# Replanning ScalarE and VectorE in a statically scheduled kernel: room kept for copies, held sums, earlier sines

## The chip, the cores and the metric

The kernel runs on one core of one Trainium2 chip. The metric is device time in microseconds (us) of one execution; lower is better. Executions are with the TensorE clock granted in full (0.999 to 1.0).

## The reference, cut to what matters

Two branches act on the same normalised input and are added to it: a state space layer (S5) with a linear recurrence over 2048 steps, and a gated MLP with a spatial product `w_sp @ z2`.

```python
xn = layernorm(x)                                    # x: 1 x 2048 x 640
# branch A: h[t] = Lam_bar * h[t-1] + B_bar @ xn[t]  (complex, 640 states)
#           y = 2 Re(C h) + xn * Dskip
# branch B: z = gelu(xn @ w_in); z1, z2 = halves of z (864 columns each)
#           z2 = layernorm(z2);  g = w_sp @ z2 + b_sp   (w_sp: 2048 x 2048)
#           out = (z1 * g) @ w_out
return x + y + branchB
```

## The kernel before

The kernel does not write its instructions in order. It records operations with what they read and write and with an expected duration. A list scheduler then fixes, before the program exists, each engine's order. That order stays as planned. In these traces an engine whose next instruction must wait does not take a later one first: below, VectorE stands idle for 3.22 us before one instruction. TensorE's order is given; that of ScalarE, VectorE and the load queue is planned.

```python
# the scheduler's choice (cut): of what can start soonest, the one with the longest tail
s0 = min(max(f, o.rdy) for o in lst)
cand = max((o for o in lst if max(f, o.rdy) <= s0 + (self.EPS0 if s0 < self.TEPS else eps)),
           key=lambda o: o.tail)
...
if op.nbytes:
    if op.lat > 2.2:                      # a transposing load
        dma_free = max(st + 1.25, dma_free) + op.nbytes / 270e3
        free[eng] = st + 0.65 + op.nbytes / 300e3
```

The products use Strassen's scheme: sums of blocks on VectorE, seven products on TensorE, and PSUM results handed on through copies on ScalarE. In the spatial stage (`W @ z2`, eight steps j) TensorE accumulates several products into one bank and needs a copy of the bank in between (shortened; each `prod` is eight matmuls, each copy an operation on ScalarE):

```python
prod(X, "A11", "B11", True, "P1")
act(copy bank X -> bank Z)                       # p1_j: P6 may not enter X before it has run
prod(Y, "S1", "T1", True, "P5")
ev(f(p5), Y, ...)                                # p5_j: P3 needs Y free
prod(X, "S2", "T2", False, "P6")
ev(f(u2), X, b0, ...)                            # u2_j: P7 may not enter X before it has run
prod(Z, "A12", "B21", False, "P2")
prod(X, "S3", "T3", False, "P7")
ev(f(u3), X, b1, ...)                            # u3_j
...
```

In the same stretch ScalarE also has to scale C (`cy`), for VectorE's products (`cp`), and the states (`P`, `Q`, `h7`), for VectorE's fixes of the recurrence (shortened):

```python
def c_scale(held):                               # at j = 3; q = 0..4
    ta, tb = cy_m[q % 2 * 2], cy_m[q % 2 * 2 + 1]     # cy of q+2 needs the buffer that cp of q reads
    act(ta = k2 * im)    # cy{q}0
    act(tb = k2 * re)    # cy{q}1
    dve(re = re * k1 + ta)   # cp{q}0
    dve(im = im * k1 - tb)   # cp{q}1
...
act(pv = sc * hv)        # P{q}{j}, Q{q}{j}: need the scan of q and its negated copy (shn{q}) from VectorE
```

The sums of blocks of W for the first step, and the sines that the recurrence needs:

```python
def s_comb(j):                                   # on VectorE
    tt(S3, a11, a21, ALU.subtract, "S3")
    tt(S1, a21, a22, ALU.add, "S1")
    tt(S2, S1, a11, ALU.subtract, "S2")
    tt(S4, a12, S2, ALU.subtract, "S4")
...
act(sins, [Civ("an"), u_m.iv()], [Civ("rn"), sin_m.iv(), cos_m.iv()], ..., "sins")
```

## Time and profile before

| | before |
|---|---|
| time, median of 3 runs | 262.41 us (262.28 to 262.89) |
| profiled execution | 262.98 us, span 260.7 us |
| TensorE busy | 256.1 us (98%) |
| first and last matmul start | 1.19 and 258.15 us |
| TensorE stalls before 30 us / after 100 us | 3.73 / 1.27 us |

"Stall" here and below means: the distance between two successive matmul starts in the trace, less N/2.4 + 2.5 ns for N columns. That is the rate which the Trainium skill gives for a warm array ("TensorE: Matmul & The Clock Gate", section "Wait — 56ns, not 53.3ns?"), and this trace agrees: 432-column matmuls follow each other every 182.5 ns and 512-column ones every 216 ns. The exception is the start: the first seven matmuls (512 columns, on zeros) follow each other every 0.40 to 0.43 us, though the granted clock reads 1.00 there. So about 1.2 us of each figure "before 30 us" is their slower pace and no wait that the change could remove. "After 100 us" sums the gaps of 0.1 us and more; "before 30 us" is all the rest. Without stalls the matmuls of this kernel take 251.97 us from the first start to the last. So the span is 1.19 us, plus 251.97 us, plus the stalls, plus a tail of about 2.56 us.

These are the busy times and the chain of work that ended last, from the page of the kernel before:

```profile
PE 256.1 (98%) x1500; PEld 151.5 (58%) x1500; DVE 243.9 (94%) x567; ACT 179.6 (69%) x323; POOL 26.0 (10%) x50
...
DVE 49%; PE 36%; POOL 4%; issue 4%; DMA 3%; ACT 1%; SPq 1%; DVEq 0%
```

TensorE is busy nearly always, but half of the chain runs through VectorE: TensorE is waiting for something that hangs on VectorE. The list "who waited for whom" of the kernel before, from 100 to 258 us, weight loads (PEld) only; columns are total us, times, longest us:

```profile
PEld ps L1079 <- ACT arena L1092: 1.6, 3, 0.7
PEld ps L1079 <- ACT ps L1101: 0.7, 1, 0.7
PEld ps L1234 <- ACT ps L1256: 0.3, 1, 0.3
PEld ps L1227 <- ACT ps L1256: 0.2, 1, 0.2
```

L1079 is the spatial product. L1101 is the copy p1 and L1092 the copies u2, c11, u3 and c21. The timeline of ScalarE at the first of these stalls (columns: start us, duration us, engine, line, operation, out<-in, count, and in brackets the idle time before and its releaser):

```profile
152.68 0.83 ACT L992 ACTIVATE arena<-arena 128x640 bf16<-128x640 bf16 x1 [0.47 <-DVE arena L997]
153.42 0.51 ACT L1101 COPY ps<-ps 128x432 f32<-128x432 f32 x1
```

ScalarE waited 0.47 us for VectorE's C product (L997), then scaled C (L992, cy20), and only then made the copy p1_4 that TensorE needed. And why VectorE was late (timeline of VectorE):

```profile
49.11 1.33 DVE L731 TENSOR_SCALAR arena<-arena 128x864 bf16<-128x864 bf16 x3
53.66 1.29 DVE L1034 TENSOR_TENSOR arena<-arena 128x1024 bf16<-128x1024 bf16 x2 [3.22 <-DMA arena<-in_B_w_sp_dram]
...
56.46 0.75 DVE L788 SCALAR_TENSOR_TENSOR arena<-arena 128x512 f32<-128x512 bf16 x1
```

It stood 3.22 us before the first sum of W (L1034), for the load of W. The recurrence (L788) began only behind that sum.

### The profile page before, as it was taken

To read this page: it belongs to the slowest core of one execution; us is meant where nothing else is said; L and a number is where in the kernel's file an instruction comes from. 1 tells how busy PE (TensorE), PEld (TensorE's weight loads), DVE (VectorE), ACT (ScalarE), POOL (GpSimd) and SP (SyncE) were. 2 spreads that over 40 slices of the span, in tenths; PEclk is the share of its full clock that TensorE was granted. 3 is DMA by queue.
4 is the path that set the end of the run, shared out by engine and by line. 5 is a ranking of instruction groups with operands and counts; after the bars stand their busy time and mean duration, and the time that the engine had idled before them with its cause. 6 is when DMAs were issued, how large, how long until landed. Compare 5 with 4: busy or idle time off the path is not lost.

```text
span 260.7 us, 4329 instructions
## 1 busy us (share of the span) xinstructions
PE 256.1 (98%) x1500; PEld 151.5 (58%) x1500; DVE 243.9 (94%) x567; ACT 179.6 (69%) x323; POOL 26.0 (10%) x50
## 2 busy tenths in 40 slices
PE   7999999999999999999999999999999999999996
PEld 3455554444446777755555544455557677777774
DVE  5899999679999999999999999999999999999953
ACT  6899999989986544533242595873979897884110
POOL 3467065400000000000000000000000000000000
PEclk9999999999999999999999999999999999999999
DMA  7946699999706962399989867893133555545641
GB/s 195 317 117 119 138 148 208 225 303 237 116 10 119 163 234 102 134 323 176 247 197 198 227 150 186 195 197 99 43 113 97 148 134 131 142 128 151 154 141 54
DMA packets 90324, 42.49 MB, mean 163 GB/s; under 512 B 73054, under 2 KB 90302, under 8 KB 90302
## 3 DMA queue, kind: packets, MB, share of 16 engines
q1 hardware_dynamic: 89982, 42.09, 67.5%
q8 instruction: 12, 0.20, 0.3%
q10 hardware_dynamic: 320, 0.12, 0.2%
q14 instruction: 10, 0.08, 0.1%
HBM read 12.28 MB, written 12.45 MB: 95 GB/s over the span
## 4 chain that ended last, share of the span: by engine, by line
DVE 49%; PE 36%; POOL 4%; issue 4%; DMA 3%; ACT 1%; SPq 1%; DVEq 0%
PE ps L1227 23%; PE ps L1079 10%; DVE arena L788 9%; DVE arena L793 5%; DVE arena L1034 5%; DVE arena L810 5%; DVE arena L790 5%; DVE arena L1013 3%; DVE arena L645 2%; DVE arena L647 2%; DVE arena L1120 2%; POOL arena L602 2%; DMA arena<-in_A_x_dram 2%; PE ps L1234 2%; DVE arena L1099 2%
## 5 line engine op out<-in xcount | busy, mean ns | idle before, releaser
L1079 PE MATMUL ps<-arena 128*128 128x432 bf16 x448 | 82.6, 346 | 0.5 <-ACT arena L1092 0.2
L1079 PEld LDWEIGHTS ps<-arena 128*128 128x128 bf16 x448 | 43.5, 98 | 39.4 <-ACT arena L1092 1.6
L1227 PE MATMUL ps<-arena 128*128 128x320 bf16 (+2 forms) x456 | 64.6, 296 | 0.0
L865 ACT ACTIVATE arena<-arena 128x512 bf16<-128x512 bf16 x70 | 46.3, 712 | 11.2 <-DVE arena L869 9.2
L1227 PEld LDWEIGHTS ps<-arena 128*128 128x128 bf16 x456 | 44.1, 98 | 17.1 <-ACT ps L1256 0.2
L665 PE MATMUL ps<-arena 128*128 128x432 bf16 x280 | 51.9, 346 | 0.1
L665 PEld LDWEIGHTS ps<-arena 128*128 128x128 bf16 x280 | 34.6, 124 | 16.4 <-DMA arena<-arena 0.5
L759 PE MATMUL ps<-arena 128*128 128x512 bf16 x200 | 43.3, 379 | 0.0
L759 PEld LDWEIGHTS ps<-arena 128*128 128x128 bf16 x200 | 19.6, 98 | 23.5 <-DMA arena<-arena 0.2
L1092 ACT ACTIVATE arena<-ps,arena 128x432 f32<-128x432 f32 (+1 forms) x32 | 19.6, 616 | 19.7 <-PE ps L1079 18.7
L788 DVE SCALAR_TENSOR_TENSOR arena<-arena 128x512 f32<-128x512 bf16 x35 | 25.7, 750 | 0.0
L764 ACT CAST arena<-ps 128x512 bf16<-128x512 f32 x40 | 22.3, 600 | 3.6 <-PE ps L759 3.5
L1034 DVE TENSOR_TENSOR arena<-arena 128x1024 bf16<-128x1024 bf16 x32 | 21.2, 691 | 3.2 <-DMA arena<-in_B_w_sp_dram 3.2
L869 DVE TENSOR_TENSOR arena<-arena 128x1024 bf16<-128x1024 bf16 (+1 forms) x42 | 24.2, 597 | 0.0
L743 ACT ACTIVATE arena<-ps 128x864 bf16<-128x864 f32 x16 | 14.2, 891 | 14.0 <-PE ps L665 11.1
L1248 DVE TENSOR_TENSOR arena<-ps,arena 128x320 bf16<-128x320 f32 (+1 forms) x40 | 18.6, 483 | 4.3 <-PE ps L1234 3.2
L810 DVE TENSOR_TENSOR arena<-arena 128x512 f32<-128x512 f32 (+2 forms) x40 | 21.6, 559 | 0.0
L1256 ACT COPY ps<-ps 128x320 f32<-128x320 f32 x24 | 9.9, 413 | 16.1 <-PE ps L1227 16.1
L793 DVE SCALAR_TENSOR_TENSOR arena<-arena 128x256 bf16<-128x256 bf16 (+1 forms) x35 | 16.8, 484 | 0.0
L790 DVE SCALAR_TENSOR_TENSOR arena<-arena 128x256 bf16<-128x256 bf16 (+1 forms) x35 | 16.8, 481 | 0.0
L1194 DVE TENSOR_TENSOR arena<-arena 128x640 bf16<-128x640 bf16 x32 | 15.3, 484 | 0.0
L1175 DVE TENSOR_TENSOR arena<-arena 128x384 bf16<-128x384 bf16 x32 | 11.1, 352 | 0.5 <-DMA arena<-g_scratch 0.5
(118 smaller groups left out, 255.4 us busy)
## 6 DMA issues: line engine op xcount, KB each, us to landing
g_scratch<-arena SPq DMA_DIRECT2D x16, 224.0 KB, 2.6
z_scratch<-arena SPq DMA_DIRECT2D x16, 216.0 KB, 1.9
arena<-z_scratch SPq DMA_DIRECT2D x8, 432.0 KB, 4.0
arena<-in_A_x_dram SPq DMA_DIRECT2D x16, 160.0 KB, 3.6
base_scratch<-arena SPq DMA_DIRECT2D x16, 160.0 KB, 2.3
arena<-base_scratch SPq DMA_DIRECT2D x16, 160.0 KB, 2.7
out_dram<-arena SPq DMA_DIRECT2D x15, 160.0 KB, 2.4
arena<-in_B_w_in_dram SPq DMA_DIRECT2D x8, 216.0 KB, 3.9
```

The costliest lines, as they stand in the source:

```text
L665: r = e.matmul(ps[:, b + h, 0:FG], lhs(k), winv[:, k, hcol * FH + h * FG:hcol * FH + (h + 1) * FG], start=(k == 0), stop=(k == ND - 1))
L759: r = e.matmul(ps[:, b, :], btv[:, ri, k, q * 128:(q + 1) * 128], xnTv[:, k, tq * 512:(tq + 1) * 512], start=(k == 0), stop=(k == ND - 1))
L764: act(lambda e: e.copy(o[:, ri, tq], ps[:, b, :].rearrange("p (m j) -> p j m", j=8)), [bank(b)], [l_m.iv((q * 8 + j) * 1024 + ri * 512 + t ...
L788: dve(lambda e: e.scalar_tensor_tensor(tv, prev, lr, cur, op0=ALU.mult, op1=ALU.add), pr + [l_iv(q, j)] + cr, [t.iv()], cd(512) + PTR, nm ...
L790: dve(lambda e: e.scalar_tensor_tensor(dst[:, 0:256], prev[:, 256:512], nli, tv[:, 0:256], op0=ALU.mult, op1=ALU.add), pr[1:2] + cr + [t.i ...
L793: dve(lambda e: e.scalar_tensor_tensor(dst[:, 256:512], prev[:, 0:256], li, tv[:, 256:512], op0=ALU.mult, op1=ALU.add), pr[0:1] + cr + [t. ...
L810: tt = lambda o, a, b, op: (lambda e: e.tensor_tensor(o, a, b, op))
L865: act(lambda e, pv=pv, hv=hv, lo=lo, sc=sc: e.activation(pv, hv[:, lo:lo + 2, 1:257], ACT.Identity, scale=sc), [h.iv(), Civ(cn)], [m.iv((q ...
L869: dve(lambda e, mv=mv, lq=lq: e.tensor_tensor(lq, lq, mv, ALU.add), li + [m.iv(0, 1024 * n)], li, cd(512 * n, 2), "fix%s%d%d" % (nm, q0, j))
L1034: dve(lambda e: e.tensor_tensor(o.ap(1024), x.ap(1024), y.ap(1024), op), [x.iv(), y.iv()], [o.iv()], cd(1024, 2), "%s_%d" % (name, j))
L1079: r = e.matmul(ps[:, bk, 0:FG], lv_[:, k, :], rv[k], start=(first and k == 0), stop=(k == 7), skip_group_check=True)
L1227: r = e.matmul(ps[:, bk, c0:c1], lf(q), rf(q)[:, c0:c1], start=(first and q == 0), stop=(q == 7), skip_group_check=True)
```

## The change

It changes no arithmetic and no instruction count; it changes orders. A second planning pass knows when each ScalarE copy for TensorE will be ready, and refuses to start another ScalarE operation that would run over it (`keep`). Operations of VectorE and ScalarE that wait for another engine are taken as ready 0.8 us later than computed (`LOOSE`). The queue time of transposing loads is set to measured values. The first sums of W may not run before the third product of the recurrence (`S_HELD`). The sines get a bias that puts them ahead of the squares, and B u takes its first token blocks later.

```diff
--- before.py
+++ after.py
@@ -31,6 +31,7 @@
 
 
     EPS0 = 0.12
+    LOOSE, LOOSE_BY = ("cy", "P", "Q", "h7", "fix"), 0.8
     TEPS = 12.0
     DMA_LAT = 2.0
     DMA_BW = 280e3
@@ -85,14 +86,29 @@
         out.sort(key=lambda s: s[0])
         self.mem[space] = out
 
+    KEEP_T0, KEEP_BY, KEEP_SLACK = 100.0, 0.25, 1.2
+
     def schedule(self):
-        ops = self.ops
-        last_pe = None
-        for op in ops:
+
+        for op in self.ops:
             for p in op.preds:
                 p.succs.append(op)
+        self.keep = []
+        self.plan()
+        for op in self.ops:
+            if op.eng == "act" and op.start > self.KEEP_T0:
+                sl = [s.start - op.done for s in op.succs if s.eng == "pe"]
+                if sl and min(sl) < self.KEEP_SLACK:
+                    self.keep.append((op.rdy, op))
+        return self.plan()
+
+    def plan(self):
+        ops = self.ops
+        keep = dict((o, r) for r, o in self.keep)
         pe = [o for o in ops if o.eng == "pe"]
         nxt = {a: b for a, b in zip(pe, pe[1:])}
+        for op in ops:
+            op.start = -1.0
         for op in reversed(ops):
             t = 0.0
             for s in op.succs:
@@ -130,6 +146,23 @@
                     cand = pe[pei]
                     st = max(f, cand.rdy)
                 else:
+                    if eng == "act" and keep:
+                        held = {}
+                        for o in lst:
+                            t = max(f, o.rdy)
+                            if o not in keep:
+                                for k, r in keep.items():
+                                    if k.start < 0 and t < r + 0.05 and t + o.occ > r + self.KEEP_BY:
+                                        t = r + k.occ
+                                        break
+                            held[o] = t
+                        s0 = min(held.values())
+                        lst2 = [o for o in lst if held[o] <= s0 + eps]
+                        cand = max(lst2, key=lambda o: o.tail)
+                        st = max(f, cand.rdy, s0 if cand not in keep else 0.0)
+                        if best is None or st < best[0]:
+                            best = (st, cand)
+                        continue
                     s0 = min(max(f, o.rdy) for o in lst)
                     cand = max((o for o in lst if max(f, o.rdy) <= s0 + (self.EPS0 if s0 < self.TEPS else eps)), key=lambda o: o.tail)
                     st = max(f, cand.rdy)
@@ -145,7 +178,7 @@
             if op.nbytes:
                 if op.lat > 2.2:
                     dma_free = max(st + 1.25, dma_free) + op.nbytes / 270e3
-                    free[eng] = st + 0.65 + op.nbytes / 300e3
+                    free[eng] = st + {163840: 1.28, 819200: 3.6}.get(op.nbytes, 1.45)
                     op.done = dma_free + 2.2
                 else:
                     at = max(st + op.occ + 0.9, dma_free)
@@ -158,6 +191,8 @@
             for s in op.succs:
                 s.npred -= 1
                 at = op.start + op.occ if eng == "pe" == s.eng else op.done
+                if eng != s.eng and s.eng in ("act", "dve") and s.name.startswith(self.LOOSE):
+                    at += self.LOOSE_BY
                 if at > s.rdy:
                     s.rdy = at
                 if s.npred == 0:
@@ -515,10 +550,11 @@
         ACTM = (0, 1, 3)
         LNE_DVE = (5, 6, 7)
         HELD = ()
-        XNB = 0.0
+        XNB = 5.0
         XN_AFTER = (6, 7, 8, 9)
         ACT_Z2 = (8, 12)
         NHALF = 4
+        SINS = 20
         XT_ACT = (6,)
         BT_AT, BT_DEP = 10, 11
         LASTN = 480
@@ -935,7 +971,7 @@
                 e.activation(C("rn"), C("an"), ACT.Sin, scale=6.2831845)
                 e.activation(s_, u, ACT.Sin, scale=-6.2831845)
                 return e.activation(c, u, ACT.Sin, scale=3.1415925)
-            act(sins, [Civ("an"), u_m.iv()], [Civ("rn"), sin_m.iv(), cos_m.iv()], 1.3 + 0.2 + 2 * 1.34 + 1.3, "sins")
+            act(sins, [Civ("an"), u_m.iv()], [Civ("rn"), sin_m.iv(), cos_m.iv()], 1.3 + 0.2 + 2 * 1.34 + 1.3, "sins", bias=SINS)
             act(lambda e: e.activation(c, c, ACT.Square, scale=math.sqrt(2.0)), [cos_m.iv()], [cos_m.iv()], ca(1280) + 0.15,
                 "tsq")
             act(lambda e: e.activation(c, c, ACT.Copy, scale=-1.0, bias=1.0), [cos_m.iv()], [cos_m.iv()], ca(1280) + 0.1,
@@ -1017,6 +1053,7 @@
             dve(tt(tv[2], b21, tv[0]), i21 + ti[0], ti[2], cd(FH, 2), "T4_%d" % n)
 
         scnt = [0]
+        S_HELD = {0: [l_iv(0, 3)]}
         s_of = {}
 
         def s_comb(j):
@@ -1031,7 +1068,7 @@
             a11, a12, a21, a22 = [w_of[(j, n)] for n in ("A11", "A12", "A21", "A22")]
 
             def tt(o, x, y, op, name):
-                dve(lambda e: e.tensor_tensor(o.ap(1024), x.ap(1024), y.ap(1024), op), [x.iv(), y.iv()], [o.iv()],
+                dve(lambda e: e.tensor_tensor(o.ap(1024), x.ap(1024), y.ap(1024), op), [x.iv(), y.iv()] + S_HELD.get(j, []), [o.iv()],
                     cd(1024, 2), "%s_%d" % (name, j))
             tt(S3, a11, a21, ALU.subtract, "S3")
             tt(S1, a21, a22, ALU.add, "S1")
@@ -1361,9 +1398,10 @@
         dve(lambda e: e.tensor_copy(bsp_m.ap(16, FP32), bsb_m.ap(16)), [bsb_m.iv()], [bsp_m.iv()], 0.08, "bsp")
         for q in range(5):
             for ri in range(2):
-                for qq in ((0, 1) if q == 0 else (q,) if q > 1 else ()):
-                    for tq in (1, 2, 3, 0):
-                        bu(qq, tq, ri)
+                for tqs in (((1, 2, 3), (0,)) if q == 0 and ri == 0 else ((1, 2, 3, 0),)):
+                    for qq in ((0, 1) if q == 0 else (q,) if q > 1 else ()):
+                        for tq in tqs:
+                            bu(qq, tq, ri)
             if q < 4:
                 t_comb(2 * q)
             for j in range(1, 8):
```

## The prediction

> **What bounds the kernel.** TensorE. It is busy 256.1 of 260.7 us, but busy time of pipelined matmuls overstates, so I read start-to-start times. Those of 432 columns follow each other every 182.5 ns, of 512 every 216 ns, of 320 every 136 ns: the N/2.4 + 2.5 ns that the Trainium skill gives for a warm array ("TensorE: Matmul & The Clock Gate", section "Wait — 56ns, not 53.3ns?"), which this trace shows. What exceeds that rate sums to only 5.0 us. Of it 3.4 us lie before 17 us, 0.2 us at 21.0 us, about 1.3 us in the second half. A tail of about 2.5 us follows the last matmul. The clock is granted in full. So the change can only win part of the 1.3 us; the start it hardly touches.
>
> **The five stalls in the second half** (the timeline): +0.39 us at 153.98, +0.19 at 157.10, +0.18 at 160.21, +0.40 at 167.92, +0.11 at 207.84; together 1.27 us. In "who waited for whom" they are weight loads of the W z2 products waiting for ScalarE's copies out of PSUM (1.6 us over 3 waits, and 0.7 us once). The cause: ScalarE did a C-scaling activation (0.82 us) first. At 152.68 it starts one, 0.47 us late for want of VectorE's C product; TensorE's copy starts only at 153.42. VectorE is late because the first sum of W waited 3.2 us for the load of W around 50 to 54 us, and is never idle from 60 to 240 us to make it good.
>
> **What the change does** (instruction order per engine; none added or removed).
> - ScalarE: three C-scalings and many state scalings P, Q and h7 move behind the copies TensorE waits for. This should remove most of the four W z2 stalls (1.16 us) and the last (0.11 us).
> - VectorE: the first sums of W now stand more than 8 us later, among the recurrence. The 3.2 us wait should vanish, and VectorE runs about 3 us earlier. That only restores the slack of the C products.
> - ScalarE: the sines (2.59 us, with a table load of 1.28 us, which agrees with "ScalarE: Activation LUTs", section "What ACT_TABLE_LOAD costs") move from 47 to about 42 us. They block PSUM copies about 3.9 us; eight banks at 1.08 us each absorb that. No TensorE time.
> - B u reorder: the first tokens' tiles are needed about 3 us later. No stall stands there, so no time.
>
> **Sum:** about −1.1 us of 1.27 us. 262.4 − 1.1 = **261.3 us**, range **260.7 to 262.3**. Faster by over 2%: 1%; within 2%: 98%; slower by over 2%: 1%.
>
> **What shows it right or wrong.** TensorE's matmul starts: the gaps near 154, 157, 160 and 168 us gone, the start of the output stage about 1.2 us earlier, the last matmul near 257 us. VectorE's wait for the load of W at 50 to 54 us gone. TensorE's waits for ScalarE's copies down from about 2.6 us to under 0.6 us. Busy times unchanged; TensorE between 40 and 110 us unchanged.
>
> **What would make it wrong.** The held copies leave ScalarE idle and push P and Q so late that VectorE's fixes miss the output products: then new stalls from 188 us on. Or the W sums, held too long, make the first spatial products late at about 110 us. Or the earlier sines starve B u of banks near 42 to 46 us. Or the start varies by more between executions than the gain (before varies by 0.6 us).

## The result, and the profile after

| | before | after |
|---|---|---|
| median of 6 runs, same rounds | 262.74 us (262.28 to 263.15) | 261.31 us (261.25 to 261.60) |
| ratio | | 0.995 (95%: 0.9937 to 0.9963) |
| profiled execution, span | 260.7 us | 259.4 us |
| TensorE stalls before 30 us | 3.73 us | 3.70 us |
| TensorE stalls after 100 us | 1.27 us | 0.00 us |
| first 320-column matmul (output stage) | 192.75 us | 191.59 us |
| last matmul start | 258.15 us | 256.85 us |

A ratio is the mean time of one kernel's runs over that of the other's of the same rounds, so it is not quite the ratio of the medians. The two profiled spans differ by 1.30 us, and the stalls by 1.27 + 0.03 us: the whole difference between these two executions is stall time of TensorE, nearly all of it after 100 us. (Four of the 200 matmuls of B u are missing from the trace of after; the four gaps of exactly one matmul that this leaves are not counted.)

The same two lines of the page of after:

```profile
PE 255.2 (98%) x1496; PEld 152.4 (59%) x1500; DVE 244.3 (94%) x567; ACT 179.8 (69%) x323; POOL 26.3 (10%) x50
...
PE 95%; DMA 3%; SPq 0%; DVE 0%; issue 0%
```

The busy share of TensorE is the same 98% as before; the chain tells the difference, because it now runs through TensorE alone. The list of waits of after has no wait of TensorE or its weight loads from 100 to 258 us, so there is nothing to show. ScalarE near 152 us in after: the copy (L1138) is ahead of the C scaling (L1028).

```profile
152.37 0.50 ACT L1138 COPY ps<-ps 128x432 f32<-128x432 f32 x1
152.78 0.83 ACT L1028 ACTIVATE arena<-arena 128x640 bf16<-128x640 bf16 x1
```

VectorE near 50 us in after: the wait for W is gone, and the recurrence (L824) starts at 51.44 us, 5.0 us earlier than before.

```profile
49.10 1.32 DVE L767 TENSOR_SCALAR arena<-arena 128x864 bf16<-128x864 bf16 x3
50.35 0.16 DVE L997 TENSOR_SCALAR arena<-arena 128x5 f32<-128x5 f32 x1
...
51.44 0.75 DVE L824 SCALAR_TENSOR_TENSOR arena<-arena 128x512 f32<-128x512 bf16 x1
```

### The profile page after: what moved, and what is told of

It is laid out like the page before. It is cut to its first block, busy times and chain, and to the rows that moved or that the text cites. A ratio compares the mean times of both kernels' runs of the same rounds, so it can differ in the third digit from the quotient of the medians.

```text
span 259.4 us, 4334 instructions
## 1 busy us (share of the span) xinstructions
PE 255.2 (98%) x1496; PEld 152.4 (59%) x1500; DVE 244.3 (94%) x567; ACT 179.8 (69%) x323; POOL 26.3 (10%) x50
## 4 chain that ended last, share of the span: by engine, by line
PE 95%; DMA 3%; SPq 0%; DVE 0%; issue 0%
PE ps L1116 32%; PE ps L1264 23%; PE ps L701 18%; PE ps L795 17%; PE ps L722 3%; DMA arena<-arena 2%; PE ps L1271 2%; DMA arena<-in_B_w_in_dram 2%; SPq L409 0%; PE ps L659 0%; DVE arena L675 0%; DVE arena L643 0%; DVE arena L1329 0%; DVE arena L633 0%
## 5 line engine op out<-in xcount | busy, mean ns | idle before, releaser
L824 DVE SCALAR_TENSOR_TENSOR arena<-arena 128x512 f32<-128x512 bf16 x35 | 25.7, 743 | 0.0
L1285 DVE TENSOR_TENSOR arena<-ps,arena 128x320 bf16<-128x320 f32 (+1 forms) x40 | 18.0, 482 | 5.3 <-PE ps L1271 3.6
L1231 DVE TENSOR_TENSOR arena<-arena 128x640 bf16<-128x640 bf16 x32 | 14.6, 482 | 0.0
L715 ACT ACTIVATE arena<-arena 128x864 bf16<-128x864 bf16 x12 | 11.1, 922 | 0.0
```

The lines of the kernel that those rows point to most:

```text
L824: dve(lambda e: e.scalar_tensor_tensor(tv, prev, lr, cur, op0=ALU.mult, op1=ALU.add), pr + [l_iv(q, j)] + cr, [t.iv()], cd(512) + PTR, nm ...
L1285: dve(lambda e: e.tensor_tensor(o[0][:, c0:c1], ps[:, bk, c0:c1], y[0][:, c0:c1], ALU.add), [bank(bk), y[1]], [o[1]], cd(c1 - c0), "%s_%d" ...
```

## The experiments

The prediction blamed ScalarE's order for the stalls, with VectorE's lateness as what had upset it. Three theories can be told apart. A: ScalarE's order alone makes the stalls. B: VectorE's lateness alone makes them. C: a stall needs both, an instruction ahead of the copy, and a VectorE late enough to hold that instruction up. Twelve kernels were run, all correct, on three chips. Each has its own runs of the kernel before (11 each), because chips may differ.

The orders were edited after planning. The helper below moves named operations in one engine's list, and then recomputes the start times, from which the waits are made:

```python
def swap(self, e, moves):
    l = self.order[e]
    for what, after in moves:
        a = next(o for o in l if o.name == what)
        l.remove(a)
        l.insert(1 + next(i for i, o in enumerate(l) if o.name == after), a)
    self.refit()
```

### Summary

The last column is the ratio to before, with its 95% interval. "Start" and "late" are TensorE's stalls before 30 us and after 100 us in the one profiled execution. "C product" is the start of VectorE's first C product, a measure of VectorE's lateness.

| kernel | chip | start | late | C product | median us | ratio to before |
|---|---|---|---|---|---|---|
| before, first profile | | 3.73 | 1.27 | 151.77 | 262.74 | |
| before again | 2 | 3.81 | 0.37 | 150.96 | 262.25 | 0.9986 (0.9959 to 1.0012) |
| before, four ScalarE moves | 1 | 3.82 | 1.49 | 152.04 | 262.29 | 1.0008 (0.9982 to 1.0033) |
| before, three VectorE moves | 1 | 3.72 | 0.33 | 150.78 | 262.27 | 1.0003 (0.9976 to 1.0030) |
| before, hold alone | 1 | 3.39 | 0.74 | 149.96 | 261.94 | 1.0001 (0.9972 to 1.0029) |
| before, sines and B u alone | 3 | 3.46 | 1.39 | 151.79 | 263.36 | 1.0033 (1.0002 to 1.0063) |
| after, first profile | | 3.70 | 0.00 | 150.28 | 261.31 | 0.995 (0.9937 to 0.9963) |
| after again | 2 | 3.92 | 0.00 | 150.51 | 261.70 | 0.9982 (0.9943 to 1.0021) |
| after a third time | 3 | 3.84 | 0.00 | 150.43 | 261.32 | 0.9951 (0.9924 to 0.9977) |
| after, one sum of W early | 1 | 3.31 | 0.85 | 151.83 | 262.58 | 1.0016 (0.9990 to 1.0041) |
| after, no room kept | 2 | 3.36 | 0.26 | 150.71 | 262.10 | 0.9988 (0.9961 to 1.0016) |
| after, no hold | 2 | 3.83 | 0.00 | 150.36 | 262.32 | 0.9986 (0.9960 to 1.0012) |
| after, sines late | 3 | 3.63 | 0.00 | 150.30 | 261.79 | 0.9982 (0.9948 to 1.0016) |
| after, tile 7 first | 3 | 3.19 | 0.00 | 149.77 | 261.12 | 0.9944 (0.9918 to 0.9969) |

The medians of before were 261.86, 262.57 and 262.39 us, with ranges of 2.1 to 2.4 us. The intervals reach about 0.26% or more to each side, so differences of under about 0.7 us between timed kernels are not established by the times; the stalls are one execution each.

The time of the C product still contains TensorE's own progress, which differs at the start. A cleaner measure of VectorE's lateness is how long after the end of ScalarE's first two C scalings VectorE begins the C product. It is 0.04 to 0.18 us in seven kernels: hold alone, the three profiles of after, no hold, sines late, tile 7 first. It is 0.62 to 0.89 us in three (three VectorE moves, before again, no room kept) and 1.61 to 2.05 us in four (before, four ScalarE moves, sines and B u alone, one sum early). The late stalls are none in the first group (0.74 us in hold alone, for a reason of its own, given in its section), 0.26 to 0.37 us in the second and 0.85 to 1.49 us in the third.

### Four ScalarE moves in the kernel before

```diff
         g.schedule()
+        g.swap("act", (("cy20", "p1_4"), ("cy31", "u2_4"), ("cy41", "u3_4"), ("Q10", "u2_5")))
```

> The kernel before with four ScalarE instructions moved one place (cy20 behind p1_4, cy31 behind u2_4, cy41 behind u3_4, Q10 behind u2_5) and nothing else. Theory A (ScalarE's order makes the four stalls): the TensorE stalls at 154, 157, 160 and 168 us go, 1.16 us in sum, and the time is 1.0 to 1.2 us under before, although VectorE's first sum of W still waits about 3.2 us for the load of W. Rival B (VectorE's lateness makes them): the stalls stay within 0.3 us of their 1.16 us, because nothing of VectorE has changed.

Measured: the copy p1_4 is now ahead (L1126 ahead of the C scaling L1017), and the three stalls at 154 to 160 us are gone although VectorE still waited 3.25 us for W. ScalarE in this kernel:

```profile
152.43 0.50 ACT L1126 COPY ps<-ps 128x432 f32<-128x432 f32 x1
152.97 0.83 ACT L1017 ACTIVATE arena<-arena 128x640 bf16<-128x640 bf16 x1
```

But the late stalls are 1.49 us, not 0.1, and the time is that of before. The lost time moved on. Here is the next meeting point at 164 to 168 us, first in the kernel before, then in this one. L830 and L855 are VectorE's negated state (shn0), L865 and L890 ScalarE's state scalings that need it, L1090 and L1115 the copy p5_5, L1092 and L1117 the copy u2_5.

```profile
164.12 0.23 DVE L830 TENSOR_SCALAR arena<-arena 128x256 bf16<-128x256 bf16 x1
...
164.38 1.33 ACT L865 ACTIVATE arena<-arena 128x512 bf16<-128x512 bf16 x2 [0.54 <-DVE arena L830]
...
165.63 0.50 ACT L1090 COPY arena<-ps 128x432 f32<-128x432 f32 x1
...
167.26 0.60 ACT L1092 ACTIVATE arena<-ps,arena 128x432 f32<-128x432 f32 x1
...
167.92 0.90 PE L1079 MATMUL ps<-arena 128*128 128x432 bf16 x4 [0.24 <-ACT arena L1092]
```

```profile
164.39 0.24 DVE L855 TENSOR_SCALAR arena<-arena 128x256 bf16<-128x256 bf16 x1
...
164.67 1.34 ACT L890 ACTIVATE arena<-arena 128x512 bf16<-128x512 bf16 x2 [1.51 <-DVE arena L855]
...
165.91 0.50 ACT L1115 COPY arena<-ps 128x432 f32<-128x432 f32 x1
...
166.93 0.61 ACT L1117 ACTIVATE arena<-ps,arena 128x432 f32<-128x432 f32 x1
...
167.60 1.09 PE L1104 MATMUL ps<-arena 128*128 128x432 bf16 x5 [0.60 <-ACT arena L1117]
```

VectorE delivers its state at about the same time in both. TensorE and ScalarE arrive 0.7 us earlier in this kernel, because they lost nothing at 154 to 160 us, and so they wait longer: ScalarE's idle time before the state scaling grows from 0.54 to 1.51 us, and the stall near 168 us from 0.40 to 0.76 us (the brackets of the PE lines give 0.24 and 0.60 us, because the ends of matmuls are modelled; the stalls are read from the starts). Two later stalls (0.26 and 0.18 us) follow in the same stage. Theory A falls as an account of the sum, while it is right about the first three stalls. Theory B's wording falls too, since those three went without any change to VectorE; but the sum stayed, as B expected.

### Three VectorE moves in the kernel before

```diff
         g.schedule()
+        g.swap("dve", (("S1_0", "h06a"), ("S2_0", "h07c"), ("S3_0", "S2_0")))
```

> The kernel before with three VectorE instructions moved (the first three sums of W for j=0, into the recurrence) and nothing else; ScalarE's order is that of before. Theory A (order alone): the 3.2 us wait for W goes, VectorE is about 2.7 us earlier, and the four stalls stay at about 1.16 us. Rival B (lateness alone) and theory C (both are needed: the old order fits a VectorE that is on time): the stalls fall under 0.3 us and the time is 1.0 to 1.2 us under before.

Measured: no wait for W; the late stalls are 0.33 us (0.20 at 166.95 and 0.13 at 206.89 us) with ScalarE's old order untouched. VectorE is earlier by 1.0 us at the C product, not by the 2.7 us expected, because it now idles for ScalarE's sines and copies at 51 to 53 us. That was enough. The time did not fall in the runs (ratio 1.0003), so the mechanism is seen here in the trace and not in the timed runs. This contradicts theory A and agrees with B and C alike; what speaks against B alone is the kernel with the four ScalarE moves. ScalarE in this kernel, with the C scaling (L1017) still ahead of the copy p1_4 (L1126):

```profile
152.11 0.82 ACT L1017 ACTIVATE arena<-arena 128x640 bf16<-128x640 bf16 x1
152.83 0.52 ACT L1126 COPY ps<-ps 128x432 f32<-128x432 f32 x1
```

### One sum of W early in the kernel after

The reads that hold the four sums back are dropped after planning, and the first sum is moved. Nothing else of any order differs from after.

```diff
         g.schedule()
+        for op in g.ops:
+            if op.name in ("S1_0", "S2_0", "S3_0", "S4_0"):
+                op.preds = {p: True for p in op.preds if p.name[:2] not in ("h0", "u0")}
+        g.swap("dve", (("S1_0", "z2n7"),))
```

> The kernel after with one VectorE instruction (the first sum of W) moved back before the recurrence, so that VectorE again waits about 3 us for the load of W; ScalarE's order stays that of after. Theory A and C: ScalarE's new order bears the late VectorE, the stalls near 154 to 168 us stay under 0.3 us in sum, and the time is within 0.4 us of after. Rival B (lateness alone): the stalls come back, about 1.2 us, and the time is that of before.

Measured: VectorE stands idle before that sum again; the profile names no DMA as releaser here ("issue"), but the trace has the third load of W landing at 52.31 us, 0.08 us before the sum starts.

```profile
52.39 0.69 DVE L1096 TENSOR_TENSOR arena<-arena 128x1024 bf16<-128x1024 bf16 x1 [2.18 <-issue]
```

The C product is at 151.83 us, as late as in before. Around 154 to 168 us only 0.15 us is lost, so there the new ScalarE order does bear the late VectorE, as A and C expected. But 0.70 us is lost after 187 us, at the output products waiting for ScalarE's copies, which no theory had expected, and the median is 0.7 us over before's of that call. Keeping room helps where the planner saw the risk; it does not make the plan proof against a late VectorE.

### The hold alone, in the kernel before

```diff
+        S_HELD = {0: [l_iv(0, 3)]}
...
-[x.iv(), y.iv()], [o.iv()],
+[x.iv(), y.iv()] + S_HELD.get(j, []), [o.iv()],
```

> The kernel before with only the hold on the first sums of W, through the scheduler (which replans ScalarE and VectorE around it). Theory B and C: stalls of the second half under 0.4 us, time 0.9 to 1.3 us under before. Theory A: stalls stay about 1.2 us unless the new plan happens to move the same copies.

Measured: no wait for W, and the earliest C product of all kernels of this call (149.96 us). Still 0.74 us of late stalls, 0.60 of it at 166.98 us. The scheduler had replanned everything around the hold: in the new order VectorE's negated state is ready at 165.04 us, later than in before (164.35 us). VectorE was on time at the C product. But shortly ahead of the negated state stands a product with z1, and it waited 1.04 us for a store to g_scratch:

```profile
163.62 0.61 DVE L1121 TENSOR_TENSOR arena<-arena 128x864 bf16<-128x864 bf16 x1 [1.04 <-DMA g_scratch<-arena]
```

In before the product at this place (L1120, at 163.27 us) did not wait. So VectorE can become late by another transfer than the load of W. One part of a plan cannot be judged by itself when the planner reacts to it. This run fits none of the expectations cleanly; it agrees with the finding that the late stalls follow the moment at which VectorE delivers what ScalarE has queued ahead of a copy.

### After, before, and two parts left out, on the second chip

After and before were run again unchanged.

> The kernel after once more, unchanged, beside the kernel before. If the gain of 1.3 to 1.4 us is the change's own: ratio 0.993 to 0.997, spread of its runs under 0.6 us, no TensorE stall after 100 us in its profile. If it was the luck of one chip or of the runs of before: ratio 0.998 to 1.002 and a spread of 1 us or more, as the kernels of the first call showed (before alone ranged from 261.14 to 263.40 us there).

> The kernel before once more, as a kernel of its own: a second profile and more runs. Ratio 0.999 to 1.001. If the stalls of the second half belong to the plan: about 1.3 us of them again near 154 to 168 us. If they depend on how late the load of W lands in an execution: another sum, larger where the first sum of W starts later than 53.7 us and smaller where it starts earlier.

Measured: after again has no late stall. Its median is 0.87 us under that of before, but one of its six runs took 264.08 us, so the interval reaches 1.0021, and the expected ratio and spread were missed; the other five lie between 261.36 and 262.14 us. Nothing shows what happened in that one run. Before again is the more instructive one. It has only 0.37 us of late stalls, and its wait for W is 2.25 us:

```profile
52.86 1.29 DVE L1034 TENSOR_TENSOR arena<-arena 128x1024 bf16<-128x1024 bf16 x2 [2.25 <-DMA arena<-in_B_w_sp_dram]
```

The program is identical to the one that lost 1.27 us. VectorE came 0.8 us earlier to its C product (150.96 against 151.77 us), and the three stalls at 154 to 160 us did not occur; the one at 167 us was 0.26 in place of 0.40 us. The load that ended the wait is the third transposing load of W, here first in before and then in before again:

```profile
50.09 1.31 SPq L372 DMA_TRANSPOSE arena<-in_B_w_sp_dram  x1
```

```profile
49.39 1.31 SPq L372 DMA_TRANSPOSE arena<-in_B_w_sp_dram  x1
```

From issue to landing it took 3.55 and 3.45 us. So 0.70 of the 0.80 us were lost before its issue: earlier transposing loads had held the queue longer (one near 37 us for 2.27 us against 1.70 us).

So the 1.27 us on which the prediction rested belonged to one execution in which W came late, not to the kernel as such. Three executions with before's ScalarE order now line up: C product at 150.78, 150.96 and 151.77 us, late stalls of 0.33, 0.37 and 1.27 us.

The kernel after without the hold, and the kernel after with one planning pass:

```diff
-        S_HELD = {0: [l_iv(0, 3)]}
+        S_HELD = {}
```

> The kernel after without the hold on the first sums of W; ScalarE still plans in two passes and keeps room. If the hold matters: VectorE waits 2 to 3.5 us for the load of W again, stalls after 100 us of 0.5 to 1.3 us, time 0.5 to 1.3 us over after. If keeping room is enough: stalls under 0.3 us and the time of after.

Measured: no late stall, and no wait for W either. The planner, which starts the sines early and knows the load times, has put the first recurrence product (51.36 us) ahead of the first sum of W (53.00 us) by itself. The hold is not needed to remove the wait. The timed runs were no better than before's (262.32 us), which the profile does not explain: its tail is 2.88 us against 2.56 us in after again, and its start is within 0.1 us. The next kernel's tail is 3.11 us; in all three VectorE's last instruction ends 0.55 us after the last matmul start, so the longer tails come after the arithmetic.

```diff
-        return self.plan()       # second pass, with room kept
+        return self.order
```

> The kernel after with a single planning pass, so that ScalarE again puts p1_4, u2_4, u3_4 behind the C-scalings; the sums of W are still held, so VectorE is on time. If VectorE's lateness was the cause: stalls after 100 us under 0.4 us, time within 0.4 us of after. If ScalarE's order was: about 1 us of stalls and the time of before.

Measured: 0.26 us of late stalls, at 195.98 us. ScalarE's three C scalings stand ahead of the copies again, as in before, and yet no stall occurs at 154 to 168 us, because VectorE is nearly on time (C product at 150.71 us, 0.89 us after the scalings):

```profile
151.78 0.82 ACT L1028 ACTIVATE arena<-arena 128x640 bf16<-128x640 bf16 x1
152.50 0.52 ACT L1138 COPY ps<-ps 128x432 f32<-128x432 f32 x1
```

This is the plainest answer to the question of cause: the old order of p1_4, u2_4 and u3_4, with a VectorE that is not far behind, costs nothing there. The 0.26 us is all that the second pass can have been worth between these two executions.

### The sines

Sines, B u order and the small bias alone, on the kernel before; and the kernel after with the sines where they were:

```diff
# sines and B u alone (on before)
-        XNB = 0.0
+        XNB = 5.0
...
-..., "sins")
+..., "sins", bias=20)
# and the B u loop of the change
# sines late (on after)
-        SINS = 20
+        SINS = 0
```

> The kernel before with only the earlier sines, the B u order and the small bias on the early transposes. What has been seen so far: the stalls after 100 us follow VectorE's lateness (before: wait for W 3.22 us, stalls 1.27 us; before again: 2.25 us, 0.37 us). If the sines are what starts VectorE's recurrence early: its first product starts near 52 to 54 us in place of 55.6 to 56.5, the first sum of W still stands before it and still waits 1 to 3 us, stalls after 100 us 0.2 to 0.8 us. If they do nothing: the stalls of before.

> The kernel after without the bias that puts the sines ahead of the squares; hold, room for copies and the new load times stay. The recurrence cannot start before the sines have ended (about 51 us), so its first product starts near 54 us, 2.5 us later than in after (51.4 to 52.1), with VectorE idle some 2 us before it. If VectorE's lateness decides: stalls after 100 us of 0.3 to 1.2 us, the time 0.3 to 1.2 us over after. If ScalarE's kept room decides: none, the time of after.

Measured, alone: the recurrence starts earlier (53.65 us), but the first sum of W still stands ahead of it and waits 1.62 us, and VectorE reaches the C product at 151.79 us, as late as before. With TensorE 0.3 us further along than in before, because it lost less at the start, the stall at 154 us is 0.74 us and the late stalls 1.39 us, above the 0.2 to 0.8 us expected. The times are 0.3% longer than before. Measured, in after with the sines late: no late stall, the C product at 150.30 us. VectorE idled only 0.8 us for the sines, and the planner had reordered the rest. So the early sines are neither enough nor needed. The sines themselves cost TensorE nothing: no kernel has a stall between 30 and 100 us. Here is ScalarE's table load for them, in before and then in after:

```profile
47.03 1.28 ACT L935 ACT_TABLE_LOAD   x1
48.32 0.27 ACT L935 ACTIVATE arena<-arena 128x80 f32<-128x80 f32 x1
```

```profile
41.92 1.28 ACT L971 ACT_TABLE_LOAD   x1
43.21 0.27 ACT L971 ACTIVATE arena<-arena 128x80 f32<-128x80 f32 x1
```

### A third time after, and an attempt to beat both

With no late stall left, what remains is the start. In every profile so far TensorE waited near 21 us for the transposing load of tile 7, by 0.07 to 0.73 us (the expectation quoted below overstates the least of them). Two neighbouring VectorE instructions are swapped in after, so that tile 7 is normalised before tile 5 is copied:

```diff
         g.schedule()
+        g.swap("dve", (("xnT5", "xn7"),))
```

> The kernel after a third time, as the measure for the other three of this call: no stall after 100 us in its profile, ratio to before 0.994 to 0.999, median 0.3 to 1.5 us under before.

> An attempt to beat both: the kernel after with two neighbouring VectorE instructions swapped near 16 us, so that the normalised tile 7 is ready about 0.4 us earlier and its transposing load is issued about 0.4 us earlier. TensorE waits 0.32 to 0.73 us at 21.0 us for that load in every run so far. Expected: that stall falls by 0.3 to 0.4 us, none appears at 17 us, the time is 0.2 to 0.4 us under after. If the load's landing is set by other traffic and not by its issue: no change.

TensorE around 21 us in after, third profile; the load (SPq) is the transpose of tiles 7 to 9, and the matmuls that wait are those of tile 7:

```profile
16.23 5.47 SPq L407 DMA_TRANSPOSE arena<-arena  x3
...
16.74 3.82 PE L701 MATMUL ps<-arena 128*128 128x432 bf16 x20
...
21.17 0.72 PE L701 MATMUL ps<-arena 128*128 128x432 bf16 x3 [0.60 <-DMA arena<-arena]
```

And with tile 7 first:

```profile
15.94 6.48 SPq L432 DMA_TRANSPOSE arena<-arena  x4
...
16.86 4.92 PE L726 MATMUL ps<-arena 128*128 128x432 bf16 x26
```

The matmuls run through without a gap. The stall of 0.77 us at 21.2 us (0.32 us in the first profile of after) is gone, none appeared at 17 us, and the start stalls are 3.19 us, the smallest of all kernels. The six runs have a median of 261.12 us against 261.32 us of after on the same chip, with overlapping ranges (260.86 to 261.35, and 260.76 to 261.72). The trace agrees with the gain, and so do the times, but neither proves it: in the thirteen other profiles, without the swap, this stall already ranged from 0.07 to 0.77 us. Of all kernels run this one has the lowest median.

## Why the prediction was right

**The bound and the size.** The forecast was 261.3 us; measured was 261.31 us. TensorE was the limit, 1.27 us of its stalls were all that the second half could give, the change removed all of them, and the start changed by 0.03 us. In the repeats the medians differed by 0.87 and 1.07 us. The exact hit has luck in it: the forecast started from 262.41 us, and before's median in the rounds of the result was 262.74 us.

**The signs.** The last matmul moved from 258.15 to 256.85 us, the output stage began 1.17 us earlier, the wait for W vanished, and TensorE's waits for ScalarE's copies after 100 us went to none. The first two were foretold within 0.2 us, and the last was under the forecast's 0.6 us. TensorE was unchanged between 40 and 110 us.

**Where the reasoning was off: the step "three C-scalings and many state scalings P, Q and h7 move behind the copies TensorE waits for. This should remove most of the four W z2 stalls".** By itself it does not. Four such moves in the kernel before took away three stalls and paid for them at the next place where ScalarE has VectorE's work queued ahead of a copy (0.76 us in place of 0.40 us at 167.6 us; 1.49 us in all). With VectorE nearly punctual, such an order cost 0.33 us in one kernel and 0.26 us in another. VectorE's lateness is what is lost; ScalarE's order decides where TensorE feels it. The prediction named the lateness as the cause behind, but gave it no worth of its own ("That only restores the slack").

**"VectorE runs about 3 us earlier".** It was 1.5 us at the C product and 2.6 us at the negated state (164.12 to 161.52 us), because VectorE also has idle time early on (1.45 us near 46 us in after, where before had 1.08 us) and its order is another. What the C product could gain was bounded as well: in after it starts 0.09 us after ScalarE's scalings, so VectorE had no more than this to win there.

**The hold.** The wait for W vanished as foretold, but the hold is not its only remedy: without it, the new plan has no wait either. With several remedies that replace each other, leaving one out shows little. The kernel after without the hold and that with the sines late both kept every late stall away.

**Variation.** The prediction took the stalls of one profile for those of the kernel. They vary: 1.27 and 0.37 us in two executions of the same program, with waits for W of 3.22 and 2.25 us. How much of the 0.87 to 1.43 us between the medians was late stalls in the runs without a profile is therefore not shown. The profiled execution of before was 262.98 us, near the slow end of its runs, so the stalls were at the high end too. After has shown none in three profiles. What part of the remaining spread of run times comes from the start (stalls of 3.2 to 3.9 us there in the profiles) is not settled, nor are the single runs of about 264 us.

## What to carry to other kernels

In a fixed order of instructions, removing one stall behind a late engine may only move the loss to the next place where its work is queued ahead of what the bottleneck needs (here 1.27 us of stalls became 1.49 us). Find the earliest idle time of the engine that is late, and give it other work there. And before you take a sum of small stalls from one profile, take a second profile of the same kernel: when the sum hangs on when the queue reaches a load, it belongs to the execution.

## What the Trainium skill lacked or had wrong

- "TensorE: Matmul & The Clock Gate", section "Wait — 56ns, not 53.3ns?", agrees with every run here after the first 6 us, for 320, 432 and 512 columns. The same page's section "Back-to-back issue gap" gives about 131 ns per matmul at 512 columns for a stream of weight loads and matmuls; here 200 such pairs followed each other every 216 ns, and no faster.
- "ScalarE: Activation LUTs", section "What ACT_TABLE_LOAD costs", gives about 1283 ns for the load and about 1380 ns more for a drain. The load took 1.28 us here. No such drain is seen: in before the load starts 0.02 us after the preceding copy ends at 47.01 us, and the first sine starts at 48.32 us.
- No page that was consulted says by how much the landing of a load varies between executions of one program. Here VectorE waited 2.25 us in one and 3.22 us in another for the same load; most of the difference was the time of issue (49.39 and 50.09 us), little the way to landing (3.45 and 3.55 us).
- "DMA: Bandwidth & Descriptors", section "DMA Transpose (X-bar)", gives no queue time for one transposing load on this chip. Here the queue was held about 1.3 us (median) by one transposing load of W, against 0.43 us by a plain store; the change set its planner to 1.45 us for a load of W (256 KB), and to 1.28 us for a 160 KB transpose, which held the queue for 1.28 us (median).
